# A spectral-mixing and MLP kernel: the first DFT in seven block products per pair of column blocks, all SBUF buffers as views of one tile

## The chip, the cores and the metric

The kernel runs on one core of a Trainium2 chip. The metric is the device time of one execution in microseconds (us). The kernel before takes 1239.16 us, the median of three runs (1237.0 to 1239.35).

The engines are named as in the profile: PE is TensorE's matmul, PEld its weight load, DVE is VectorE, ACT is ScalarE, POOL is GpSimd, SP is SyncE, which issues most of the DMAs.

## The reference

The input x has 2048 rows (S) of 576 (D); the hidden width is 4608. A layer norm feeds two branches, whose results are added to x:

```python
a = jnp.einsum("bsd,ed->bse", x, dft_hid_re)
b = jnp.einsum("bsd,ed->bse", x, dft_hid_im)
y = jnp.einsum("ts,bse->bte", dft_seq_re, a) - jnp.einsum("ts,bse->bte", dft_seq_im, b)
...
h = jnp.einsum("bsd,df->bsf", x, w1)
h = jnp.maximum(h, zero)
return jnp.einsum("bsf,fd->bsd", h, w2)
...
return x + _A_ref(xn, ...) + _B_ref(xn, B_w1, B_w2)
```

The first two lines are the first DFT (over the 576 columns), the third is the second DFT (over the 2048 rows).

## The kernel before

**Arithmetic.** Every float32 operand is scaled by a power of two and split into a high and a low float16 part (`split`: ACT writes the high half, DVE the low one). A product of two matrices is then three float16 products: high by high, high by low, low by high. Where "seven products" are spoken of, a matrix product is cut into 2 x 2 blocks and made of seven block products instead of eight, with sums of blocks made ahead on DVE and sums of results made behind (P1 to P7 in the code).

**Stages.** First come loads, norm and transposes (`xT`: x transposed, float16 high and low, for four groups g of 512 rows). Then the MLP: nine blocks b of 512 hidden columns, each over the four groups; one pair (b, g) is a step. In each step the first layer (L559) and the previous step's second layer (`mlp2`, L665: seven products of 24 matmuls of 288 columns) run on TensorE. ACT and DVE take the results of `mlp2` out of PSUM into sum buffers (L676, L680), and POOL issues a DMA that adds them to a spill in DRAM (L683). In the last block, the sum buffers are `sums`.

The first DFT follows: `dft1(t)` for 16 tiles t of 128 rows, each with four column blocks j of 288 (real columns in two halves, imaginary ones in two). For each tile there are 13 full matmuls for each j (L1252) and a product of 64 rows for what 576 leaves beyond 4 x 128 (L1262, for two tiles at once). The four results lie in four PSUM banks, and the next tile uses four others. ACT and DVE then make of them the operands R of the second DFT: the blocks b11, b21 and b22 and the four sums T1 to T4, each in a high and a low half (L1272 to L1284). The four blocks of the DFT matrix D have a scale each (`scales_d`, `rho`).

The second DFT is 16 units (p, kh) of seven products with 24 matmuls each (L1381): p is a pair of output tiles, kh the half of the 2048 rows that is summed over. Its left operands come from the matrix C (`load_c`: four transfers of 512 KB a unit), split by `operand` three products ahead of use. For the scale of C the absolute values of all its blocks are summed earlier (`first_c`, `sum_c`: a pass over C, one block at a time behind the MLP); four of the 64 blocks are counted during the first DFT instead (`count_c`).

**Order.** `todo` and `work` are a list of small tasks (weights of the next block: load, maximum, scale, splits, sums), taken one by one between the products. `ends` is a list of the last MLP step's remaining conversions. A Tile scheduler puts the instructions on their engines; `behind`, `issue_after` and the order of the code decide what stands behind what.

Buffers come from pools; a pool released and another one opened reuse the same memory, and the later buffer waits for what was in it.

Of the kernel before, what the change touches and what calls it, by code (L numbers as in the profile page):

```python
# [41 lines left out]

BB = 2
# [6 lines left out]
def kernel(  # L50
# [22 lines left out]
    accp = tc.alloc_tile_pool(name="accp", bufs=1)  # L73
    raw = tc.alloc_tile_pool(name="raw", bufs=2)
    mlp = tc.alloc_tile_pool(name="mlp", bufs=2)
    dpool = tc.alloc_tile_pool(name="dpool", bufs=1, side="right")
    xpool = [tc.alloc_tile_pool(name=f"xpool{g}", bufs=1, side="right") for g in range(NG)][::-1]
    ps1 = tc.alloc_tile_pool(name="ps1", bufs=4, space=PSUM)
# [3 lines left out]
    dbuf = dpool.tile([P, 4 * 5 * EH], F32, name="dbuf")  # L82
# [3 lines left out]
    acct = accp.tile([P, NG, TG, D], F32, name="acc")  # L86
    accs = [acct[:, g] for g in range(NG)]
# [9 lines left out]
    stage = mlp.tile([P, 5, NQ, GH], F32, name="stage", bufs=1)  # L97
# [7 lines left out]
    def load_raw(key, src, shape):  # L105
        r = raws[key] = raw.tile(shape, F32, tag="raw", name="raw_" + "_".join(map(str, key)))
        ins = nc.sync.dma_start(r, src).ins
        if key[:2] == ("w2", 1):
            order["loads"] = ins

    def load_w1(b, i, parts=1):
        if b:
            r = raw.tile([P, 2 * KT, P], F32, tag="raw", name=f"raw_w1_{b}_{i}")
        else:
            r = stages[i].rearrange("p (k f) -> p k f", f=P)
# [84 lines left out]
    xT = [xpool[g].tile([P, NKX + 1, G], F16, name=f"xT{g}") for g in range(NG)]  # L200
# [150 lines left out]
    w1bufs = [mlp.tile([P, W1B], F32, name=f"w1buf{i}", bufs=1) for i in range(2)]  # L351
# [37 lines left out]
    def new_h(b, g, i):  # L389
        if i == 0:  # L390
            h = mlp.tile([P, 2, 7, NQ, GH], F16, tag="h", name=f"h{b}_{g}")
# [56 lines left out]
    flats = acct.rearrange("p g a b -> p g (a b)")  # L448
    flat = [flats[:, g] for g in range(NG)]
# [5 lines left out]
    every = acct.rearrange("p g a b -> p (g a b)")  # L455
    cbufs = [
        every[:, k * TG * D - GH : k * TG * D + GH].rearrange("p (i t) -> p i t", i=NQ) for k in (1, 3)
# [180 lines left out]
    sumbufs = [mlp.tile([P, 2, EH], F32, name="sum0", bufs=1)] + [  # L638
# [151 lines left out]
    def new_w2(b, i):  # L790
        w2s[b, i] = mlp.tile([P, 2, 7, EH], F16, tag="w2s", name=f"w2s{b}_{i}", bufs=4)
# [222 lines left out]
    dsp = None  # L1014

    rho = []
    PARTS_D = (slice(0, 3), slice(3, KT))

    def load_d(j):
        load_raw(("d", j), dft[:, :, j * EH : (j + 1) * EH], [P, KT, EH])  # L1020

    def max_d(j, c):

        if j == c == 0:
            sc["d"], pw["d"], mx["d"] = cell("sd", 4), cell("pd", 4), cell("md", 4)
        if c == 0:
            mx["dp"] = cell("mdp", 2)
        with tc.issue_after(order["vfree"]):
            magnitude(mx["dp"][:, c : c + 1], raws["d", j][:, PARTS_D[c]])
        if c:  # L1030
            nc.vector.tensor_reduce(mx["d"][:, j : j + 1], mx["dp"], AX.X, ALU.max)

    def power_d(j):
        m = slice(j, j + 1)
        yield from power(sc["d"][:, m], pw["d"][:, m], mx["d"][:, m])

    def new_d():
        nonlocal dsp
        dsp = [d.bitcast(F16).rearrange("p (n k e) -> p n k e", n=2, k=KT) for d in dbufs]

    def split_d(j, c):
        k = PARTS_D[c]
        with behind("free"), behind("vfree"):
            split(dsp[j][:, 0, k], dsp[j][:, 1, k], raws["d", j][:, k], sc["d"][:, j : j + 1])

    def scales_d():

        top, inv = cell("pdm", 1), cell("pdi", 1)
        nc.vector.tensor_reduce(top, pw["d"], AX.X, ALU.max)
        nc.vector.tensor_scalar(  # L1050
            inv.bitcast(I32), top.bitcast(I32), EXPONENT, None, ALU.bitwise_xor
        )
        r = cell("rho", 5)
        for n, (j, sign) in enumerate(((0, 1), (1, 1), (2, -1), (3, -1), (0, -1))):
            rho.append(r[:, n : n + 1])
            nc.vector.tensor_scalar(
                rho[n], pw["d"][:, j : j + 1], inv, sign * 0.25, ALU.mult, ALU.mult
            )
        pw["d"] = top
# [5 lines left out]
    units = [(p, kh) for p in range(NP) for kh in range(2)]  # L1065
# [9 lines left out]
    def first_c(m):  # L1075
        n, q = divmod(m, 4)
        f = firsts[m] = mlp.tile([P, HK, P], F32, tag="first", name=f"f{n}_{q}", bufs=1)
# [3 lines left out]
    def sum_c(m):  # L1081
# [10 lines left out]
        lambda m=m: (sum_c(m - 1) if m > 4 else None, first_c(m)) for m in range(4, 4 * len(units))  # L1092
# [4 lines left out]
    for n in range(2, len(steps)):  # L1097
        b, g = steps[n]
        pb, pg = steps[n - 1]
        if g == 0 and b:  # L1100
            if b + 1 < NB:
                todo += prepare_block(b + 1)
            else:
                todo += [lambda: (load_d(0), load_d(1)), lambda: None, new_d, lambda: None]
                for j in range(4):
                    d = power_d(j)
                    todo += [lambda j=j: max_d(j, 0), lambda d=d, j=j: (max_d(j, 1), next(d))]
                    todo += [lambda: None, lambda d=d: later(d)]
                    todo += [lambda j=j, c=c: split_d(j, c) for c in range(2)]
                    if j < 2:  # L1110
# [338 lines left out]
```

## Time and profile before

| what | us |
|---|---|
| median of three runs | 1239.16 |
| lowest, highest | 1237.0, 1239.35 |
| profiled execution, its own time | 1238.39 |
| its span (first to last instruction) | 1236.6 |
| stretch of the MLP looked at, blocks in full swing | 440 to 760 |
| the last MLP products, and the first of the first DFT | 784.3 to 797.5 |
| the first DFT | 797.5 to 903.6 |
| the second DFT | 903.6 to 1234.0 |

The granted clock of TensorE is 1.00 in the profiled execution. In the tables of stretches each engine's column is its busy time inside the stretch with its number of instructions in brackets; then come the clock, the mean busy share of the 16 DMA engines and the GB/s that they moved. A row of the groups by form has the busy time of all, the mean of one in ns, and behind the bar the idle time of the engine ahead of them with its releasers. A row of the chain has the start, the duration and what ran. A row of the timeline has the start, the duration and the instruction, with the idle time ahead of it in square brackets.

### The profile page before, as it was taken

The numbers are of one execution on the slowest core, as the hardware profiler recorded it, in microseconds if no ns is written. First come the engines' busy times: TensorE is split into PE (matmuls) and PEld (weight loads), VectorE is DVE, ScalarE is ACT, GpSimd is POOL, SyncE is SP. The second block draws the span as 40 slices with busy tenths as digits, with TensorE's granted clock in tenths as the row PEclk, the third lists the DMA queues.
The fourth block names the chain that finished last, engine by engine and source line by source line (L and its number), as shares of the span: only waits on it lengthen the run. The fifth ranks groups of instructions, "written<-read, shape, count | busy, mean of one in ns | idle before, by whom it ended". The sixth has DMA issues, their size and how long they took to land.

```text
span 1236.6 us, 24680 instructions
## 1 busy us (share of the span) xinstructions
PE 1221.1 (99%) x10269; PEld 965.6 (78%) x10269; DVE 988.3 (80%) x1639; ACT 696.1 (56%) x1024; POOL 158.8 (13%) x208
## 2 busy tenths in 40 slices
PE   8999999999999999999999999999999999999998
PEld 7665657888888888888888888777777777777776
DVE  8998899778877788878877877476887878787875
ACT  5655456676675676666767666445543333333332
POOL 2431211111121212121211111200000000000000
PEclk9999999999999999999999999999999999999999
DMA  8994546657565667576566666620054344433420
GB/s 314 210 162 98 85 70 141 129 125 156 123 141 137 151 132 142 113 157 123 126 149 146 153 134 136 128 69 1 1 175 146 117 130 133 144 119 133 129 88 20
DMA packets 80320, 157.25 MB, mean 127 GB/s; under 512 B 22224, under 2 KB 41168, under 8 KB 80208
## 3 DMA queue, kind: packets, MB, share of 16 engines
q1 hardware_dynamic: 57424, 113.20, 29.4%
q0 software_dynamic: 22784, 42.48, 23.5%
q8 instruction: 80, 1.31, 0.4%
q14 instruction: 32, 0.26, 0.1%
HBM read 104.53 MB, written 51.90 MB: 127 GB/s over the span
## 4 chain that ended last, share of the span: by engine, by line
PE 78%; DVE 11%; issue 5%; DMA 2%; ACT 2%; POOL 1%; SPq 0%; POOLq 0%; ACTq 0%; DVEq 0%
PE p L1381 27%; PE p L665 21%; PE bank L559 19%; PE pd L1252 8%; PE p L356 1%; PE bank L578 1%; DVE h L431 1%; DVE w2s L196 1%; DMA raw_w<-in_w_dram 1%; POOL spill L683 1%; DVE w1buf L196 1%; DMA spill<-sums 1%; DVE h L414 1%; DVE st L219 1%; DVE acc L491 1%
## 5 line engine op out<-in xcount | busy, mean ns | idle before, releaser
L665 PE MATMUL p<-w2s,h 128*128 128x288 f16 x3024 | 399.1, 286 | 4.7 <-DVE acc L680 2.7
L665 PEld LDWEIGHTS <-h 128*128 128x128 f16 x3024 | 295.7, 98 | 81.8 <-issue 6.0
L1381 PE MATMUL p<-R,cs 128*128 128x288 f16 x2688 | 329.4, 286 | 0.0
L1381 PEld LDWEIGHTS <-cs 128*128 128x128 f16 x2688 | 263.0, 98 | 66.3
L195 ACT ACTIVATE cs<-c,sc_c 128x1024 f16<-128x1024 f32 x112 | 125.2, 1144 | 196.7 <-DVE c L1314 72.6
L196 DVE SCALAR_TENSOR_TENSOR cs<-c,sc_c,cs 128x1024 f16<-128x1024 f32 x112 | 141.0, 1282 | 54.4 <-ACT cs L195 54.4
L559 PEld LDWEIGHTS <-w1buf 128*128 128x128 f16 x1476 | 143.0, 98 | 22.5 <-issue 4.4
L559 PEld LDWEIGHTS <-dbuf 128*128 128x128 f16 x1104 | 107.0, 98 | 16.1 <-issue 2.5
L1252 PE MATMUL pd<-dbuf,xT 128*128 128x288 f16 x832 | 104.0, 286 | 0.0
L594 DVE TENSOR_TENSOR h<-stage,h 128x1024 f16<-128x1024 f32 x56 | 68.4, 1223 | 42.2 <-ACT h L590 42.2
L559 PE MATMUL bank<-acc,w1buf 128*128 128x256 f16 x768 | 97.8, 273 | 0.8 <-ACT acc L611 0.8
L1252 PEld LDWEIGHTS <-xT 128*128 128x128 f16 x832 | 80.8, 98 | 22.0 <-issue 1.9
L559 PE MATMUL bank<-xT,w1buf 128*128 128x256 f16 x708 | 95.8, 273 | 0.0
L683 POOL DMA_DIRECT2D spill<-dbuf x70 | 60.6, 872 | 248.0 <-DVE dbuf L680 237.9
L585 ACT ACTIVATE h<-acc 128x512 f16<-128x512 f32 x56 | 35.2, 629 | 75.8 <-DVE acc L615 40.0
L559 PE MATMUL bank<-acc,dbuf 128*128 128x256 f16 x576 | 73.3, 273 | 0.0
L559 PE MATMUL bank<-xT,dbuf 128*128 128x256 f16 x528 | 71.5, 273 | 0.0
L1387 DVE SCALAR_TENSOR_TENSOR o<-p,us_c,o 128x288 f32<-128x288 f32 x112 | 57.5, 513 | 12.9 <-PE p L1381 12.5
L1086 ACT ACTIVATE f<-f 128x1024 f32<-128x1024 f32 x60 | 62.8, 1047 | 3.0 <-DMA f<-in_cre_dram 1.8
L683 POOL DMA_DIRECT2D spill<-sum x42 | 37.3, 889 | 196.1 <-DVE sum L680 172.1
L676 ACT ACTIVATE dbuf<-p,c_ub 128x576 f32<-128x576 f32 x70 | 51.1, 732 | 16.1 <-PE p L665 16.1
L590 ACT ACTIVATE h<-stage 128x1024 f16<-128x1024 f32 x56 | 58.7, 1050 | 0.0
(170 smaller groups left out, 1507.1 us busy)
## 6 DMA issues: line engine op xcount, KB each, us to landing
spill<-dbuf POOLq DMA_DIRECT2D x70, 288.0 KB, 5.8
c<-in_cre_dram SPq DMA_DIRECT2D x32, 512.0 KB, 4.0
c<-in_cim_dram SPq DMA_DIRECT2D x32, 512.0 KB, 4.8
f<-in_cre_dram SPq DMA_DIRECT2D x30, 512.0 KB, 5.1
f<-in_cim_dram SPq DMA_DIRECT2D x30, 512.0 KB, 4.8
spill<-sum POOLq DMA_DIRECT2D x42, 288.0 KB, 4.3
raw_w<-in_w_dram SPq DMA_DIRECT2D x18, 576.0 KB, 4.8
raw_w<-in_w_dram SPq DMA_DIRECT2D x16, 640.0 KB, 5.6
```

The source lines that it names most:

```text
L195: nc.scalar.activation(hi, src, AF.Copy, scale=s).ins,
L196: nc.vector.scalar_tensor_tensor(lo, src, s, hi, ALU.mult, ALU.subtract).ins,
L559: nc.tensor.matmul(ps[:, i], l, r, start=first and i == m == 0, stop=m == len(todo) - 1, skip_group_check=not first or i > 0,)
L590: order["s"] = nc.scalar.activation(h[:, 0, S1 + 2 * i :][:, :2], stage[:, 1 + 2 * i :][:, :2], AF.Copy).ins
L594: order["lo"] = nc.vector.tensor_tensor(lo, stage[:, 1 + 2 * i :][:, :2], hi, ALU.subtract).ins
L665: order["pe"] = nc.tensor.matmul(ps[:, c], h[:, x, qa, c * P : (c + 1) * P], w[:, y, qb], start=first and i == 0 and j == 0, stop=i == NQ ...
L676: freed(nc.scalar.activation(o, ps, AF.Copy, scale=us[b]))
L683: nc.gpsimd.dma_start(spill[g, row, col], o, accum_op=ALU.add)
L1086: nc.scalar.activation(f, f, AF.Abs, scale=2.0**-10, accum_out=sums_c[:, n, q : q + 1])
L1252: nc.tensor.matmul(ps[j], xT[g][:, kx, c * P : (c + 1) * P], dsp[j][:, hl, k], start=(t % 2 == 0 and n == 0), stop=(t % 2 == 1 and n == le ...
L1381: nc.tensor.matmul(ps, w[:, a, k], r[:, c, rq], start=first and k == 0 and j == 0, stop=k == HK - 1 and j == 2, skip_group_check=not first,)
L1387: order["o"] = nc.vector.scalar_tensor_tensor(o, ps, us["c"][:, n : n + 1], o, ALU.mult, ALU.add).ins
```

## The change

**One tile for all buffers.** The pools for SBUF are gone. One tile, `arena`, holds everything; each buffer is a view at an offset worked out by hand (`spots`, `words`), and rings of buffers are taken in turn (`turn`). What waits for what is decided by overlapping ranges, so a later buffer can lie over an earlier one as soon as that is read.

**The first DFT in rounds.** `dft1` is replaced by eight rounds s = (g, c). A round takes two tiles of 128 rows (k = 0, 1) and, for each of two pairs e of column blocks (real, imaginary), seven block products in place of eight. The products stand in PSUM in `U0` and `U1` (one bank each: P1, then P6, then P7, then P4, of e = 0 and of e = 1), `W0` or `W1` (two banks: P5, then P3) and `V` (two banks: P2):

```python
def place(s, e, q):
    if q in (P2, P5, P3):
        return PS["V" if q == P2 else f"W{s % 2}"][:, e]
    return PS[f"U{e}"][:, 0]
def take(s, what, e):
    ...
    if what in ("v", "w", "u"):
        order["dv"] = nc.vector.scalar_tensor_tensor(dst, src, SCALE, dst, ALU.mult, ALU.add).ins
    else:
        order["da"] = nc.scalar.activation(dst, src, AF.Copy, scale=SCALE).ins
```

`take` empties them into a float32 buffer X of the round: c11, r21, c22 and c21 by ACT, and u, w and v are added to what stands there by DVE. `convert` makes R of X: for each of the two tiles the high halves h1, h2, h3a, h3b by ACT, the sums t13, t2, t4 by DVE, the low halves l1, l2 by DVE and l3a, l3b by POOL:

```python
def lo(a, b):
    tt = (nc.gpsimd if a.start > 2 or late_r else nc.vector).tensor_tensor
    tt(r[:, 1, a], x[:, b], r[:, 0, a], ALU.subtract)
```

Part of a round's conversions is made in the next round ("one" is tile k = 1 of this round, "old" the same tile's rest in the next, "late" is tile k = 0 of the round before). The order on the engines is written out as a list and pinned:

```python
else:
    seq = (
        (P1, 0), ("c11", 0), ("late", "h1"), (P1, 1), ("c11", 1), ("old", "t4"), ("old", "l3b"),
        ("old", "h3a"), ("late", "l1"), ("late", "h2"), (P5, 0), ("old", "l3a"), ("late", "l2"),
        ("late", "t13"), (P6, 0), ("r21", 0), ("late", "t2"), ("late", "t4"), (P5, 1),
        ("c22", None), (P6, 1), ("r21", 1), ("late", "h3b"), ("late", "h3a"), (P7, 0), ("u", 0),
        ("late", "l3b"), (P3, 0), (P7, 1), ("u", 1), ("late", "l3a"), ("m", 0),
        (P3, 1), ("rest", 0), ("w", None), ("m", 1), ("m", 2), (P4, 0), ("c21", 0), ("one", "h1"),
        ("one", "l1"), (P4, 1), ("c21", 1), ("one", "h2"), ("one", "l2"), ("one", "t13"), ("one", "t2"),
        (P2, 0), (P2, 1), ("v", None), ("one", "h3b"),
    )
```

("rest" are the eight products of 64 rows, `drests`; "m" stands in the last round alone: the first two operands of the second DFT and one pair of sums of C.)

**The junction.** In round 0 the list alternates with the last MLP step: P1 of e = 0, the MLP's product 0, P5, product 1, P6, product 2, P7, product 3, P3, product 4, P1 of e = 1, product 5, P5, product 6.

**D.** All of D has one scale (and its negative). Its blocks are loaded in two pairs, the second pair twice, six loads of 720 KB in place of four. DVE makes sums of its blocks, and each pair is split into 17 parts of 288 columns in high and low.

**The rest.** The pass over C counts all 64 blocks behind the MLP, with an added place for it in each block's second step; `count_c` is gone. The units of the second DFT come as (0,0), (1,0), (1,1), (0,1), then as before. The last pair's conversions are made in the first unit, two after each product, with all their low halves on POOL.

The diff, cut:

```diff
+    arena = const.tile([P, 4 * W2W + 2 * (HW + RW) + FW + SW + KW + 2 * W1B + 32 + DW + NG * (AW + XW) + 32], F32, name="arena")
...
-    def max_d(j, c):
...
+        r = cell("sd", 2)
+        sc["d"], pw["d"] = [r[:, e : e + 1] for e in range(2)], cell("pd", 1)
+        yield from power(sc["d"][0], pw["d"], m)
+        nc.vector.tensor_scalar(sc["d"][1], sc["d"][0], -1.0, None, ALU.mult)
...
-    units = [(p, kh) for p in range(NP) for kh in range(2)]
+    units = [(0, 0), (1, 0), (1, 1), (0, 1)] + [(p, kh) for p in range(2, NP) for kh in range(2)]
...
-        lambda m=m: (sum_c(m - 1) if m > 4 else None, first_c(m)) for m in range(4, 4 * len(units))
+        lambda m=m: (sum_c(m - 1) if m else None, first_c(m)) for m in range(4 * len(units))
...
-    for q in range(7):
-        mlp2(*steps[-1], q)
-        for _ in range(2):
-            if ends:
-                ends.pop(0)()
...
-        for n, (kx, hl, k) in enumerate(XK[:-1]):
-            for j in range(4):
-                nc.tensor.matmul(
-                    ps[j], xT[g][:, kx, c * P : (c + 1) * P], dsp[j][:, hl, k],
-                    start=(t % 2 == 0 and n == 0), stop=(t % 2 == 1 and n == len(XK) - 2),
-                )
...
+    def dproduct(s, e, q):
+
+        g, c = divmod(s, 2)
+        ps = place(s, e, q)
+        x, a = [y[:, :, c * P : (c + 1) * P] for y in right(g, q)], LEFT[q]
+        first = q in (P1, P2, P5) and (s, e, q) not in opened
+        todo = [
+            (x[z][:, k], dsp(e, y, a + k)) for k in range(2) for y, z in ((0, 0), (1, 0), (0, 1))
+        ]
+        if q in REST:
+            k, t = REST[q]
+            lows = q in (P2, P5) and (s, e, q) not in opened
+            todo += [
+                (xT[g][:, KM, (2 * t + c) * P :][:, :P], dsp(e, y, k)) for y in range(1 + lows)
+            ]
+        for m, (l, r) in enumerate(todo):
+            nc.tensor.matmul(
+                ps, l, r, start=first and m == 0, stop=m == len(todo) - 1,
+                skip_group_check=not first,
+            )
...
+        elif n > 2 and kh and units[n + 1 :]:
+            load_out(units[n + 1][0])
...
+            for _ in range(2):
+                if rest_r:
+                    rest_r.pop(0)()
```

How the change stands on the engines: ACT first. Of the first DFT before, the five instructions of one tile (t = 1); `pd1_0` to `pd1_3` are its four banks, `c12` and `T` float32 buffers, `R1` the operand:

```order
L1272 ACTIVATE c12_1_9825<-pd1_1_9745,c_rho_9375 128x288
L1280 ACTIVATE R1_9771<-pd1_0_9744,c_rho_9375 128x288
L1280 ACTIVATE R1_9771<-pd1_3_9747,c_rho_9375 128x288
L1280 ACTIVATE R1_9771<-pd1_2_9746,c_rho_9375 128x288
L1283 ACTIVATE R1_9771<-T1_9824 128x1152
```

ACT now, in round 2 from its start: U0 (c11 of e = 0), h1 of the late tile, U1 (c11 of e = 1), h3a of the old tile, h2 of the late tile, U0 (r21), W (c22), U1 (r21), h3b and h3a of the late tile, U0 (c21), h1 of this round's tile, U1 (c21). All buffers in SBUF have the one name `arena`:

```order
L1348 ACTIVATE arena_63<-U0_9375 128x288
L1359 ACTIVATE arena_63<-arena_63 128x576
L1348 ACTIVATE arena_63<-U1_9376 128x288
L1359 ACTIVATE arena_63<-arena_63 128x576
L1359 ACTIVATE arena_63<-arena_63 128x288
L1348 ACTIVATE arena_63<-U0_9375 128x288
L1348 ACTIVATE arena_63<-W0_9374 128x576
L1348 ACTIVATE arena_63<-U1_9376 128x288
L1359 ACTIVATE arena_63<-arena_63 128x576 x2
L1348 ACTIVATE arena_63<-U0_9375 128x288
L1359 ACTIVATE arena_63<-arena_63 128x576
L1348 ACTIVATE arena_63<-U1_9376 128x288
```

What moved: an eviction (from U or W) used to follow its own tile's others; now conversions of two other tiles stand between the evictions of one round.

DVE in the first DFT. Before, the eight instructions of tile t = 2:

```order
L1274 SCALAR_TENSOR_TENSOR T2_9908<-pd2_0_9840,c_rho_9375,c12_2_9909 128x288
L1275 SCALAR_TENSOR_TENSOR T2_9908<-pd2_3_9843,c_rho_9375,c12_2_9909 128x288
L1276 SCALAR_TENSOR_TENSOR T2_9908<-pd2_3_9843,c_rho_9375,T2_9908 128x288
L1281 SCALAR_TENSOR_TENSOR R2_9839<-pd2_0_9840,c_rho_9375,R2_9839 128x288
L1277 SCALAR_TENSOR_TENSOR T2_9908<-pd2_2_9842,c_rho_9375,T2_9908 128x288
L1281 SCALAR_TENSOR_TENSOR R2_9839<-pd2_3_9843,c_rho_9375,R2_9839 128x288
L1281 SCALAR_TENSOR_TENSOR R2_9839<-pd2_2_9842,c_rho_9375,R2_9839 128x288
L1284 TENSOR_TENSOR R2_9839<-T2_9908,R2_9839 128x1152
```

And now, round 3 from the late tile's l1 (l1, l2, t13, t2, t4, then the additions u of U0 and U1 and w of W1, then l1, l2, t13 and t2 of the round's own tile):

```order
L1363 TENSOR_TENSOR arena_63<-arena_63 128x576
L1363 TENSOR_TENSOR arena_63<-arena_63 128x288
L1367 TENSOR_TENSOR arena_63<-arena_63 128x2x288
L1375 TENSOR_TENSOR arena_63<-arena_63 128x288
L1376 TENSOR_TENSOR arena_63<-arena_63 128x288
L1346 SCALAR_TENSOR_TENSOR arena_63<-U0_9375,arena_63 128x288
L1346 SCALAR_TENSOR_TENSOR arena_63<-U1_9376,arena_63 128x288
L1346 SCALAR_TENSOR_TENSOR arena_63<-W1_9575,arena_63 128x576
L1363 TENSOR_TENSOR arena_63<-arena_63 128x576
L1363 TENSOR_TENSOR arena_63<-arena_63 128x288
L1367 TENSOR_TENSOR arena_63<-arena_63 128x2x288
L1375 TENSOR_TENSOR arena_63<-arena_63 128x288
```

What moved: the additions from PSUM stand behind five pieces of the round before, and a value is added to in SBUF instead of being worked out from four banks.

POOL, from its last spills to the program's end. Before, one reduction over partitions (for C's scale) ends its work:

```order
L683 DMA spill3_00_107<-sums_8825 128x576
L683 DMA spill3_11_110<-sums_8825 128x576
L683 DMA spill3_01_108<-sums_8825 128x576
L683 DMA spill3_10_109<-sums_8825 128x576
L133 ISA top_10314<-max_c_10312 128x16
L1445 UNCONDITIONAL_BRANCH
L1445 ISA
```

And now:

```order
L717 DMA spill3_01_83<-arena_63 128x576
L717 DMA spill3_10_84<-arena_63 128x576
L1363 ISA
L1363 TENSOR_TENSOR arena_63<-arena_63 128x576 x29
L1363 TENSOR_TENSOR arena_63<-arena_63 128x288 x2
L1363 TENSOR_TENSOR arena_63<-arena_63 128x576 x5
```

What moved: the reduction for C's scale stands ahead of the last seven spills, and behind the last spill come a change of POOL's library (the ISA row) and the 36 low halves.

More of the change, by code (lines that the diff above doesn't have):

```diff
@@ L1133 @@
             t_sum = lambda q: next(tq, None)
+            more = lambda q: g == 1 and count(q)
             rest = lambda q: rests(n + 1 if n + 1 < len(steps) else None)
@@ new lines, with drests @@
+    opened = set()
+    def drests(items):
+        for m, (s, e, q) in enumerate(items):
+            g, c = divmod(s, 2)
+            ps = place(s, e, q)
+            r, kx = m % 2, (KM, NKX)[m % 2]
+            rows = slice(r * REM, (r + 1) * REM)
+            k, t = REST[q]
+            opened.add((s, e, q))
+            nc.tensor.matmul(
+                ps, xT[g][rows, kx, (2 * t + c) * P :][:, :P], dsp(e, 1, k)[rows],
+                start=q in (P2, P5), stop=True, skip_group_check=q not in (P2, P5),
+            )
```

422 lines of the change are left out of this document (262 added, 160 removed).

## The prediction

> **What bounds the kernel now.** I read the page's busy times and its chain first, then a table of stretches, one for each stage, then the chain around the first DFT.
>
> ```profile
> PE 1221.1 (99%) x10269; PEld 965.6 (78%) x10269; DVE 988.3 (80%) x1639; ACT 696.1 (56%) x1024; POOL 158.8 (13%) x208
> PE 78%; DVE 11%; issue 5%; DMA 2%; ACT 2%; POOL 1%; SPq 0%; POOLq 0%; ACTq 0%; DVEq 0%
> ```
>
> ```profile
> core 0: us, PE busy (x) PEld busy (x) DVE busy (x) ACT busy (x) POOL busy (x), PEclk, DMA share, GB/s
> 440.00:760.00 320.00, 320.00 (x2811) 265.93 (x2808) 254.01 (x424) 215.75 (x341) 56.03 (x72) 1.00 0.66 141
> 760.00:784.30 24.30, 23.48 (x204) 19.27 (x202) 18.50 (x35) 14.87 (x24) 4.61 (x7) 1.00 0.52 97
> 784.30:797.50 13.20, 12.29 (x100) 9.47 (x98) 5.71 (x7) 5.89 (x8) 3.52 (x5) 1.00 0.74 136
> 797.50:903.60 106.10, 106.10 (x886) 82.05 (x885) 75.28 (x131) 55.99 (x91) 1.99 (x3) 1.00 0.12 33
> 903.60:1234.00 330.40, 329.32 (x2689) 262.82 (x2686) 261.58 (x290) 123.60 (x113) 0.00 (x0) 1.00 0.38 125
> ```
>
> TensorE is the bound in every stage: 320.00 of 320.00 us in the late MLP blocks, 106.10 of 106.10 in the first DFT, 329.32 of 330.40 in the second. The clock is 1.00 throughout. So a matmul that is left out is worth its full time, and a wait that is put in costs its full time. The one gap beside the change is the junction, 784.3 to 797.5, where 0.9 us of TensorE is idle. The chain shows it and the price of a product:
>
> ```profile
> 730.78 2.94 PE p L665 x24
> ...
> 785.63 8.06 DMA spill<-sums
> ...
> 793.80 0.75 ACT sums L676
> ...
> 794.59 3.10 PE p L665 x24
> 797.69 4.78 PE pd L1252 x39
> 802.47 0.60 PE pd L1262 x8
> 803.07 12.85 PE pd L1252 x104
> ...
> 897.17 6.48 PE pd L1252 x52
> 903.64 329.29 PE p L1381 x2688
> ```
>
> ```profile
> PE p L665 <- ACT sums L676: 0.7, 1, 0.7
> PE p L665 <- ACT h L590: 0.2, 1, 0.2
> ```
>
> A full product costs 12.85/104 = 0.1236 us in the first DFT, a rest product 0.60/8 = 0.075 us.
>
> **What is removed.** The order of instructions has 738 full products in place of 832 and 62 rests in place of 64; up to the junction TensorE's order is the same in both. So 94 x 0.1236 = 11.62 us and 2 x 0.075 = 0.15 us leave a stage that has no idle time: **-11.77**.
>
> **Pace.** Before, successive products go to four banks in turn. Now six or seven in a row stay in one bank, as in the MLP's second layer (2.94/24 = 122.5 ns) and the second DFT (329.29/2688 = 122.5). If that sets the pace, 738 x 1.1 ns = 0.8 us; if not, 0. I take **-0.8**, because these groups are nearest in form.
>
> **Junction.** 0.67 us of the idle time ends with an ACT eviction that waited for a spill of 8.06 us, 0.25 us with an ACT piece of h. Now 47 of the first round's products (5.8 us) stand between the last seven MLP products and need neither. Bounds: 0 to -0.9; I take **-0.9**. The first round's own evictions fall due several microseconds after their products there, so it adds no wait that I can find.
>
> **What is added.** Work per round, of which rounds 1 to 7 have 92 x 0.1236 + 8 x 0.075 = 11.97 us of TensorE:
>
> ```profile
> L195 ACT ACTIVATE w2s<-raw_w,c_sw 128x576 f16<-128x576 f32 x36 | 26.5, 767 | 3.9 <-DVE raw_w L786 2.3 <-DVE raw_w L788 1.4
> L1280 ACT ACTIVATE R<-pd,c_rho 128x288 f16<-128x288 f32 x48 | 24.0, 501 | 21.4 <-DVE T L1274 11.0 <-DVE T L1277 5.2 <-DVE T L1276 5.2
> L605 DVE TENSOR_TENSOR h<-stage,h 128x512 f16<-128x512 f32 x28 | 19.1, 684 | 0.7 <-ACT h L604 0.5
> L280 POOL TENSOR_TENSOR dbuf<-dbuf 128x512 f16<-128x512 f32 x11 | 12.8, 1163 | 0.0
> L676 ACT ACTIVATE sums<-p,c_ub 128x576 f32<-128x576 f32 x16 | 11.8, 736 | 10.4 <-PE p L665 8.6 <-DMA spill<-sums 1.8
> L680 DVE SCALAR_TENSOR_TENSOR sums<-p,c_ub,sums 128x576 f32<-128x576 f32 x12 | 9.8, 813 | 7.5 <-ACT sums L676 3.9 <-PE p L665 3.6
> L786 DVE TENSOR_TENSOR raw_w<-raw_w 128x288 f32<-128x288 f32 x18 | 8.1, 452 | 0.2
> L1276 DVE SCALAR_TENSOR_TENSOR T<-pd,c_rho,T 128x288 f32<-128x288 f32 x16 | 8.1, 508 | 0.0
> ```
>
> ACT: six evictions of 288 (6 x 0.50), one of 576 (0.74), six high halves of 576 (6 x 0.77) and two of 288 (about 0.5 each): 9.4 us. DVE: two additions from PSUM of 288 (0.51), two of 576 (0.81), four SBUF pieces of 576 (0.684 x 576/512 = 0.77) and six of 288 (0.45): 8.4 us. POOL: four low halves of 576, 1.163 x 576/512 = 1.31 each, 5.2 us. No engine is full against 11.97 us, so only order can hurt.
>
> **The new wait.** Two banks, U0 and U1, each take P1, P6, P7 and P4 in turn, so each product but the first needs the eviction of the one before. Before, eight banks went round and nothing had to be empty so soon. From the end of a product to its eviction, and along a chain of ACT and DVE, this part of the trace has:
>
> ```profile
> 856.17 0.67 PE L1262 MATMUL pd<-dbuf,xT 64*128 64x288 f16 x8
> 856.57 0.50 ACT L1272 ACTIVATE c<-pd,c_rho 128x288 f32<-128x288 f32 x1 [1.73 <-PE pd L1262]
> ...
> 859.36 0.50 ACT L1280 ACTIVATE R<-pd,c_rho 128x288 f16<-128x288 f32 x1 [0.35 <-DVE T L1277]
> ```
>
> The eviction at 856.57 reads what the second of eight rests finished at 856.17 + 0.15, so 0.25 us lie between. I laid a round's instructions on the four engines with these durations, counted from its start. P1 ends at 0.74 and 1.48, P6 of the first half ends at 3.09 and of the second at 4.70; P7's first is due at 4.70 into the bank that P6's eviction (r21) frees. P6's first itself waits for the eviction of P1: ACT has it at 1.8 to 2.3, just in time for 2.35, because the previous round's h pieces stand ahead of it. ACT then has two high halves of the previous pair ahead of r21 and ends it at about 4.9: **0.2 us late**. P3 next is due at 5.4 and needs one eviction that ends at 5.5, which the delay covers. The rests are due at 7.9 and need DVE's additions of P7, done at 7.99: nothing more. So +0.2 in seven rounds: **+1.4**. Bounds: 0 if ACT's starts overlap as they do in this trace's rows, and 0.85 a round (+6) if ACT's pieces each cost a 0.35 us start as at 859.36 and two of them stand ahead of r21.
>
> **POOL's new task.** Before its first low half POOL changes its library. The only such gap is
>
> ```profile
> 49.63 0.56 POOL L964 PARTITION_ALL_REDUCE none<-eps  x1 [5.90 <-issue]
> ```
>
> 5.9 us after the last spill is issued (about 802) gives 808; the first low half is wanted by round 1, near 808, and its result only by the second DFT, nearly 100 us later. Cost 0; if the cover failed, X's first half would be rewritten late and one round would wait 2 to 3 us.
>
> **D and its sums.** DVE's splits (34 parts), maxima (8) and seven sums in the last block come to about 23 us, as much as the preparation of an ordinary block's weights, and such blocks run at 320.00 of 320.00. Two more loads of 720 KB fall where the DMA share is 0.52. Cost 0. In block 0 a few pieces of ACT and DVE change places; TensorE has 0.3 us idle there, so I allow 1 us either way:
>
> ```profile
> 60.00:80.00 20.00, 19.67 (x140) 13.50 (x139) 19.44 (x50) 11.84 (x21) 5.42 (x5) 1.00 0.95 136
> ```
>
> **Start of the second DFT.** The last pair's conversions go into the first unit, whose DVE has
>
> ```profile
> 904.00:924.60 20.60, 20.60 (x171) 16.46 (x169) 18.32 (x24) 8.44 (x10) 0.00 (x0) 1.00 0.83 263
> ```
>
> 18.3 us and gets 3.3 more (two pieces of 0.77 and four of 0.45), 21.6 for 20.6. The operands run three products (72 x 0.1225 = 8.8 us) ahead, which swallows 1 us of backlog. Converted rows of the last pair are read one unit later, since the units are reordered. Cost 0; up to +5 if POOL's low halves hold DVE up.
>
> **Sum.** 1238.39 (the profiled execution; its span is 1236.6) - 11.77 - 0.8 - 0.9 + 1.4 = 1226.3. The median of the three runs is 0.77 above that execution, so the forecast is **1227**.
>
> **A rule that speaks against it.** Two rows of block 0 show DVE held by POOL:
>
> ```profile
> 18.56 0.14 DVE L234 SCALAR_TENSOR_TENSOR u<-mv,r 128x2 f32<-128x2 f32 x1
> 23.92 1.16 POOL L280 TENSOR_TENSOR dbuf<-dbuf 128x512 f16<-128x512 f32 x1
> 24.27 0.82 DVE L234 SCALAR_TENSOR_TENSOR u<-mv,r 128x4 f32<-128x4 f32 x1
> ```
>
> The same small operation takes 0.14 us alone and 0.82 us when it begins inside a POOL piece, and both end together at 25.08. The Trainium skill, "SBUF — State Buffer", section "SBUF: two separate sides", says that the port pair shared by the two engines is an exclusive lock, so that a DVE operation with two SBUF inputs waits for the whole of a GpSimd one; the trace agrees with 0.82 against 0.14.
>
> **The rivals.** (1) Everything is hidden, no wait at r21: 1238.39 - 13.5 + 0.8 = 1225.7. For it: ACT's pieces in this trace overlap by 0.1 us each; against: r21's slack is negative on paper.
>
> (2) DVE and POOL exclude each other, and DVE becomes the chain of the round. Then 8.4 + 5.2 = 13.6 us, and with a start of 0.35 us at some two of its hand-overs 14.3, stand against 11.97: 2.3 us a round, 16 in seven, and 1238.39 - 13.5 + 16.3 + 0.8 = **1242, slower**. It decides from 13.5/7 = 1.9 us of wait a round. For it: the rows above. Against: DVE's pieces that read PSUM have one SBUF input only, the low halves are wanted by nobody within the round, and POOL's four pieces start when ACT's halves are done, which leaves DVE free in between.
>
> (3) The second DFT starts late: DVE's backlog, POOL's locks and 2 MB of C with the spilled rows arrive together. 5 us on the forecast, 1232. For it: 0.83 of the DMA there already; against: three products of lead.
>
> (4) The change does not bring its count: the products would have to take 832 x 123.6/738 = 139 ns to give back all. Nothing in the trace is near it; 1239.
>
> **How the numbers follow.** Forecast 0.61 (own range 1224.5 to 1230), (1) 0.13, (3) 0.14, (2) 0.09, (4) 0.03. About 0.2 per cent, 2.5 us, is the least that a measurement of this kernel tells from no change. Faster: 0.61 + 0.13 + 0.14 = 0.88; same 0.03; slower 0.09. The range goes from 1224 (all bounds low and block 0 a little better) to 1236 (0.85 us a round, or a late second DFT with more than 5): that leaves out (2), (4) and little else.
>
> **What would show it.** Right: 738 full products at about 122.5 ns, rounds of 12.1 to 12.2 us, a wait of 0.2 us in each before P7, named ACT; no idle TensorE near 788 and 794; the second DFT still at 329 of 330. Wrong: waits of a microsecond or more before the rests, named DVE, with DVE pieces stretched beside POOL ones (rival 2); idle TensorE within 20 us after the last round (rival 3); idle in the MLP's blocks, which I hold to be untouched.

## The result, and the profile after

| | before | after |
|---|---|---|
| median of 20 runs | 1239.16 | 1237.97 |
| lowest, highest | 1237.0, 1240.55 | 1235.75, 1239.27 |
| span of the profiled execution | 1236.6 | 1235.9 |

The ratio is 0.999 (95% interval 0.9983 to 0.9996): 1.2 us faster, where 12.2 were forecast (1227). The time lies above the range's upper end, 1236.

First the page of the kernel after, the busy times:

```profile
PE 1211.0 (98%) x10173; PEld 956.2 (77%) x10173; DVE 999.4 (81%) x1619; ACT 707.2 (57%) x1073; POOL 210.2 (17%) x241
```

TensorE does 10.1 us less (1221.1 before), 96 matmuls fewer, and the span is only 0.7 us shorter: nearly all of the gain came back as idle time of TensorE. The table of stretches says in which stages (the columns are as before):

```profile
760.00:784.30 24.30, 20.95 (x181) 17.16 (x179) 18.00 (x26) 15.20 (x24) 3.46 (x4) 1.00 0.61 140
784.30:797.50 13.20, 13.03 (x108) 10.30 (x106) 10.22 (x15) 6.80 (x13) 3.97 (x5) 1.00 0.52 82
...
903.60:1234.00 330.40, 324.30 (x2641) 258.18 (x2639) 264.47 (x289) 121.89 (x112) 10.13 (x5) 1.00 0.35 116
```

From 760 to 784.3 TensorE is idle for 3.4 us (0.8 before), from 903.6 on for 6.1 us (1.1 before); 1.4 and 1.1 us of these lie behind the last product. The junction is nearly full. The single waits are in TensorE's timeline of the kernel after (start, duration, instruction, idle time ahead and its releaser; only the rows with a wait are shown):

```profile
775.19 1.47 PE L593 MATMUL bank<-arena 128*128 128x256 f16 x12 [1.07 <-ACT arena L647]
782.04 0.40 PE L612 MATMUL bank<-arena 64*128 64x256 f16 x4 [2.29 <-DVE arena L649]
791.06 1.63 PE L699 MATMUL p<-arena 128*128 128x288 f16 x12 [0.17 <-DVE arena L714]
821.00 0.28 PE L1328 MATMUL U<-arena 64*128 64x288 f16 x1 [0.16 <-DVE arena L1346]
897.66 6.04 PE L1555 MATMUL p<-arena 128*128 128x288 f16 x48 [0.50 <-ACT arena L1348]
905.16 6.04 PE L1555 MATMUL p<-arena 128*128 128x288 f16 x48 [1.45 <-DVE arena L1561]
911.86 3.10 PE L1555 MATMUL p<-arena 128*128 128x288 f16 x24 [0.67 <-DVE arena L1561]
916.44 3.10 PE L1555 MATMUL p<-arena 128*128 128x288 f16 x24 [1.48 <-DVE arena L1561]
920.11 17.80 PE L1555 MATMUL p<-arena 128*128 128x288 f16 x144 [0.57 <-DVE arena L1561]
938.41 294.16 PE L1555 MATMUL p<-arena 128*128 128x288 f16 x2400 [0.50 <-DVE arena L1561]
```

The rounds themselves hold no wait but the 0.16 us at 821. The sum of the two profiled executions closes so: work -11.77; junction -0.75 (0.92 to 0.17); rounds +0.16; last MLP block +2.5 (1.07 + 2.29 against 0.82); start of the second DFT +5.2 (the last six rows; none before); waits ahead of 500 us +2.4 (12.37 against 9.94, of which more below); and some 0.16 us for each of nine more restarts after a wait (a row of 48 ahead of a wait lasts 6.04 where 48 x 0.1225 is 5.88), +1.4. Together -0.8; the spans differ by 0.7.

**The second DFT's start.** DVE and POOL in the first unit, two timelines of the kernel after, DVE's first:

```profile
893.84 2.03 DVE L230 SCALAR_TENSOR_TENSOR arena<-arena,sc_c 128x1024 f16<-128x1024 f32 x1 [1.05 <-ACT arena L229]
...
897.65 2.29 DVE L1409 TENSOR_TENSOR arena<-arena 128x1024 f32<-128x1024 f32 x1
...
919.98 1.87 DVE L230 SCALAR_TENSOR_TENSOR arena<-arena,sc_c 128x1024 f16<-128x1024 f32 x1
```

```profile
892.27 2.52 POOL L1363 TENSOR_TENSOR arena<-arena 128x576 f16<-128x576 f32 x2 [2.27 <-ACT arena L1359]
897.39 4.82 POOL L1363 TENSOR_TENSOR arena<-arena 128x576 f16<-128x576 f32 x3 [2.60 <-ACT arena L1359]
...
912.85 7.92 POOL L1363 TENSOR_TENSOR arena<-arena 128x576 f16<-128x576 f32 x4 [7.04 <-ACT arena L1359]
```

Without POOL beside them the same two operations of DVE take 1.27 and 1.21 us (quoted below). The one at 893.84 takes 0.76 us more and ends at 895.87, which is 1.08 us after POOL's pair ends (892.27 + 2.52 = 894.79). The one at 919.98, of the same form, ends at 921.85, again 1.08 us after POOL's last piece (912.85 + 7.92 = 920.77). Though they lie beside POOL's piece for 0.95 and 0.79 us, nearly all of their work, 1.08 of 1.27 us, is done behind it; engines that only slowed each other down would have done a part of it before (as far as POOL's spans, which are rough, tell). The one at 897.65 ends at 899.94; if POOL's first of three took 1.26 us, as each of the pair at 892.27 did, it ended at 898.65, and 1.29 us are left for DVE's. POOL waits too: four pieces in a row take 7.92 us, 1.98 each, against those 1.26.

**The last MLP block.** The second load of D's imaginary columns, ACT's timeline of the kernel after, and three rows of DVE's:

```profile
770.92 1.01 ACT L229 ACTIVATE arena<-arena,c_sd 128x864 f16<-128x864 f32 x1 [3.46 <-DMA arena<-in_dft_dram]
...
778.64 0.78 ACT L229 ACTIVATE arena<-arena,c_sd 128x576 f16<-128x576 f32 x1 [2.55 <-DMA arena<-in_dft_dram]
779.32 0.61 ACT L619 ACTIVATE arena<-arena 128x512 f16<-128x512 f32 x1
```

```profile
764.48 0.81 DVE L230 SCALAR_TENSOR_TENSOR arena<-arena,c_sd 128x576 f16<-128x576 f32 x1
...
767.13 0.81 DVE L230 SCALAR_TENSOR_TENSOR arena<-arena,c_sd 128x576 f16<-128x576 f32 x1
...
781.30 0.68 DVE L649 TENSOR_TENSOR arena<-bank,arena 128x512 f32<-128x512 f32 x1
```

ACT stands still for 3.46 and 2.55 us with a split of D at its head, and behind it stand the pieces of h (L619) that DVE's eviction L649 comes after; TensorE's 2.29 us end with that eviction. The load could not start before 765.4 and 768.0, since it goes where the real columns lie until they are split: DVE's splits at 764.48 and 767.13 end at 765.29 and 767.94. SP's timeline shows its issues right behind, with one block of C between them, and the chain what the second took:

```profile
765.36 0.55 SPq L141 DMA_DIRECT2D arena<-in_dft_dram  x1
765.96 0.62 SPq L1132 DMA_DIRECT2D arena<-in_cre_dram  x1
767.97 0.55 SPq L141 DMA_DIRECT2D arena<-in_dft_dram  x1
```

```profile
767.97 10.64 DMA arena<-in_dft_dram
```

That is the longest of D's six loads, whose median is 7.4 us. So the second wait of ACT has two parts, a late start and a slow transfer.

### The profile page after: what moved, and what is told of

Its sections match the earlier page's. It is cut to its first block, busy times and chain, and to the rows that moved or that the text cites. A ratio compares the mean times of both kernels' runs of the same rounds, so it can differ in the third digit from the quotient of the medians.

```text
span 1235.9 us, 24513 instructions
## 1 busy us (share of the span) xinstructions
PE 1211.0 (98%) x10173; PEld 956.2 (77%) x10173; DVE 999.4 (81%) x1619; ACT 707.2 (57%) x1073; POOL 210.2 (17%) x241
## 3 DMA queue, kind: packets, MB, share of 16 engines
q8 instruction: 79, 1.29, 0.4%
## 4 chain that ended last, share of the span: by engine, by line
PE 73%; DVE 15%; issue 5%; ACT 3%; DMA 3%; POOL 0%; SPq 0%; ACTq 0%; POOLq 0%; DVEq 0%
PE p L1555 24%; PE p L699 22%; PE bank L593 19%; DVE arena L230 3%; PE U L1312 3%; PE W L1312 2%; DMA arena<-in_w_dram 1%; PE p L392 1%; DVE arena L714 1%; PE bank L612 1%; ACT arena L229 1%; DVE arena L468 1%; DMA arena<-in_dft_dram 1%; PE V L1312 1%; DVE arena L451 1%
## 5 line engine op out<-in xcount | busy, mean ns | idle before, releaser
L699 PE MATMUL p<-arena 128*128 128x288 f16 x3024 | 400.2, 286 | 5.8 <-DVE arena L714 5.7
L699 PEld LDWEIGHTS <-arena 128*128 128x128 f16 x3024 | 295.8, 98 | 83.5 <-issue 8.4
L1555 PE MATMUL p<-arena 128*128 128x288 f16 x2688 | 330.2, 286 | 5.2 <-DVE arena L1561 4.7
L1555 PEld LDWEIGHTS <-arena 128*128 128x128 f16 x2688 | 263.0, 98 | 72.4 <-issue 6.3
L593 PE MATMUL bank<-arena 128*128 128x256 f16 x2580 | 304.8, 273 | 1.2 <-ACT arena L647 1.1
L593 PEld LDWEIGHTS <-arena 128*128 128x128 f16 x2580 | 250.1, 98 | 39.1 <-issue 7.6
L229 ACT ACTIVATE arena<-arena,sc_c 128x1024 f16<-128x1024 f32 x112 | 124.3, 1144 | 199.5 <-DVE arena L1410 75.3
L717 POOL DMA_DIRECT2D spill<-arena x144 | 128.6, 911 | 553.4 <-DVE arena L714 504.5
L230 DVE SCALAR_TENSOR_TENSOR arena<-arena,sc_c 128x1024 f16<-128x1024 f32 x112 | 144.3, 1312 | 51.8 <-ACT arena L229 51.8
L710 ACT ACTIVATE arena<-p,c_ub 128x576 f32<-128x576 f32 x144 | 105.5, 734 | 43.3 <-PE p L699 38.2
L230 DVE SCALAR_TENSOR_TENSOR arena<-arena,c_sw 128x640 f16<-128x640 f32 (+2 forms) x118 | 98.2, 847 | 24.8 <-ACT arena L229 24.5
L229 ACT ACTIVATE arena<-arena,c_sw 128x640 f16<-128x640 f32 (+3 forms) x118 | 90.3, 795 | 23.1 <-DVE c_sw L171 10.8
L392 PE MATMUL p<-arena 128*128 128x128 f16 (+1 forms) x680 | 98.5, 300 | 1.8 <-ACT arena L347 1.1
L1312 PEld LDWEIGHTS <-arena 128*128 128x128 f16 x738 | 71.6, 98 | 19.7 <-issue 1.9
L392 PEld LDWEIGHTS <-arena 128*128 128x128 f16 x680 | 52.3, 98 | 40.3 <-issue 3.8
L619 ACT ACTIVATE arena<-arena 128x512 f16<-128x512 f32 x56 | 35.2, 628 | 67.7 <-DVE arena L649 39.7
```

The lines of the kernel that those rows point to most:

```text
L229: nc.scalar.activation(hi, src, AF.Copy, scale=s).ins,
L230: nc.vector.scalar_tensor_tensor(lo, src, s, hi, ALU.mult, ALU.subtract).ins,
L392: order["m1"] = nc.tensor.matmul(ps[:, cols], w1s[b, i // 2][:, hl, i % 2 * KT + k], xT[g][:, kx, cols], start=(start and n == 0), stop=(s ...
L593: nc.tensor.matmul(ps[:, i], l, r, start=first and i == m == 0, stop=m == len(todo) - 1, skip_group_check=not first or i > 0,)
L699: order["pe"] = nc.tensor.matmul(ps[:, c], h[:, x, qa, c * P : (c + 1) * P], w[:, y, qb], start=first and i == 0 and j == 0, stop=i == NQ ...
L710: freed(nc.scalar.activation(o, ps, AF.Copy, scale=us[b]))
```

## The experiments

Theory 1: at the start of the second DFT, DVE has more than it can do, and POOL's hold on it is the larger part. Theory 2: in the last MLP block ACT and DVE wait, at the head of their queues, for a load that starts late. Theory 3: the extra slot of the pass over C costs about 1 us in the earlier blocks. The rivals: plain work of DVE for 1 and 2, and differences from execution to execution for 3.

**u1_late**: the last pair's conversions in the second unit.

```diff
-            for _ in range(2):
+            for _ in range(4 if n == 1 else 0):
                 if rest_r:
-                    rest_r.pop(0)()
+                    with tc.issue_after(order["o"]), tc.issue_after(order["oa"]):
+                        rest_r.pop(0)()
```

(`order["oa"]` is ACT's half of the last operand's split, so that the pieces keep their place on ACT too. In the kernel after nothing pins the pieces: its code has 14 of the 22 behind the first unit's products and eight behind the second's, but on the engines all stand in the first unit, where POOL's last ends at 920.77.)

> The last pair's conversions (22 pieces) move from the first unit of the second DFT, two after each product, to the second unit, four after each product; nothing is left out. Theory 1 (in the first unit DVE has more than it can do: the pieces themselves and the low halves on POOL, which hold DVE's operations up): TensorE's idle time in the first unit falls from 5.2 us to under 1 us, and the time from 1238.0 to about 1232.5 (5.2 us of idle time and some 0.16 us for each of the five restarts). Rival (the operands are late for another reason, such as C's loads or the spilled rows): 3 us or more of idle time stay in the first unit, and the time is 1236 or more.

Measured 1238.16, ratio to before 0.9991 (0.9982 to 0.9999): no gain over the kernel after (1237.97). But the waits moved with the pieces. TensorE's timeline and the stretches of u1_late:

```profile
932.71 3.10 PE L1555 MATMUL p<-arena 128*128 128x288 f16 x24 [1.11 <-DVE arena L1561]
937.58 8.98 PE L1555 MATMUL p<-arena 128*128 128x288 f16 x72 [1.77 <-DVE arena L1561]
948.28 8.98 PE L1555 MATMUL p<-arena 128*128 128x288 f16 x72 [1.72 <-DVE arena L1561]
957.75 4.45 PE L1555 MATMUL p<-arena 128*128 128x288 f16 x35 [0.50 <-DVE arena L1561]
```

```profile
900.00:921.00 21.00, 20.30 (x165) 15.94 (x164) 18.06 (x22) 8.62 (x9) 1.21 (x1) 1.00 0.46 146
921.00:942.00 21.00, 18.11 (x147) 14.13 (x146) 17.66 (x21) 8.84 (x11) 12.22 (x8) 1.00 0.29 101
```

The first unit now loses 0.6 us; the second loses 2.9 (the first two rows) and the third, whose operands are made beside the last pieces, 2.2. So C's loads are not the cause, since the first unit still has them; the pieces are. The expectation's 1232.5 was wrong in taking the second unit to have room for them.

**u0_nolow** and **u0_nosums** part the pieces. The first leaves out the eight low halves on POOL, the second DVE's six sums:

```diff
-            tt(r[:, 1, a], x[:, b], r[:, 0, a], ALU.subtract)
+            if not late_r:
+                tt(r[:, 1, a], x[:, b], r[:, 0, a], ALU.subtract)
```

```diff
-    rest_r = [d[k] for d in (old, late) for k in keys]
+    rest_r = [d[k] for d in (old, late) for k in keys if k[0] != "t"]
```

> The eight low halves of the last two tiles, which POOL writes in the first unit of the second DFT, are left out; the other 14 pieces stay where they are. If POOL's hold on DVE is the larger part of theory 1: DVE's operands in the first unit take 1.2 to 1.3 us each again in place of 1.6 to 2.3, idle time at most 1.5 us, time about 1233 to 1234. If DVE's own added sums (3.3 us) are the larger part: 3 us or more of idle time stay and the time is 1236 or more.

> The six sums t13, t2, t4 of the last pair (3.3 us of DVE) are left out, the low halves on POOL stay. Theory 1a (POOL's hold on DVE is the larger part): 2 to 3.5 us of the 5.2 us of idle time in the first unit stay, 1235 to 1236.5. Theory 1b (it is the sum of both that overflows, and either alone fits): idle time under 1.5 us, time 1232 to 1233.5.

Measured 1231.76 (ratio 0.9939, 0.9925 to 0.9952) and 1237.59 (0.9987, 0.9978 to 0.9997). TensorE's waits at the start of the second DFT, from the list of waits of u0_nolow, and from the timeline of u0_nosums:

```profile
PE p L1556 <- ACT arena L1348: 0.5, 1, 0.5
PE p L1556 <- DVE arena L1562: 0.5, 1, 0.5
```

```profile
898.79 6.04 PE L1555 MATMUL p<-arena 128*128 128x288 f16 x48 [1.51 <-ACT arena L1348]
907.36 6.04 PE L1555 MATMUL p<-arena 128*128 128x288 f16 x48 [2.53 <-DVE arena L1561]
914.17 3.10 PE L1555 MATMUL p<-arena 128*128 128x288 f16 x24 [0.77 <-DVE arena L1561]
917.92 2.24 PE L1555 MATMUL p<-arena 128*128 128x288 f16 x17 [0.66 <-DVE arena L1561]
```

Without POOL's pieces 1.0 us is left of 5.2; without DVE's 3.3 us of sums 5.5 us is left, more than theory 1a asked for, and 1237.59 lies above the ranges of both 1a and 1b. The sums alone are not the loss; the hold makes nearly all of it. In u0_nosums the low halves also come in another order: all eight run in one string of 14.39 us on POOL, beside DVE's operands.

**u01_dve** and **u01_spread**: nothing left out, the 22 pieces spread over two units, with the pins of u1_late; in the first DVE makes the low halves, in the second POOL still does. They differ in that line alone.

```diff
-            for _ in range(2):
+            for _ in range((1, 1, 1, 2, 2, 2, 2)[i] if n == 0 else 2):
...
-            tt = (nc.gpsimd if a.start > 2 or late_r else nc.vector).tensor_tensor
+            tt = (nc.gpsimd if a.start > 2 and not late_r else nc.vector).tensor_tensor
```

> Nothing is left out. The last pair's low halves are made by DVE instead of POOL (5.5 us more of DVE, no hold), and the 22 pieces are spread over the first two units of the second DFT. By the durations of the rows DVE has 2 x 16.6 + 3.3 + 5.5 = 42 us for 41.2: idle time of 1 to 2.5 us, time 1238.0 - 3 to 4.5 = 1233.5 to 1235. If the hold were not the matter: as u1_late, 1237 to 1238.5.

> Nothing is left out. The 22 pieces are spread over the first two units, the low halves still on POOL. Theory 1 with a hold of up to 1.3 us for each of eight POOL pieces: DVE has 33.2 + 3.3 + 6 to 10 = 42.5 to 46.5 us for 41.2, idle time 1.5 to 5 us, 1234 to 1238. Rival (only the bunching in one unit matters): idle time under 1 us, 1232.5.

Measured 1233.29 (0.9953, 0.9936 to 0.9969) and 1237.65 (0.999, 0.9981 to 0.9999). The first gives DVE some 5.4 us more work than the second gives it (six pieces of 0.75 us and two of 0.44), and is 4.4 us faster: TensorE waits 1.1 us at the start of its second DFT, 5.4 us in u01_spread. So bunching alone is not the cause either; spread out, POOL's pieces cost as much. Stretches of 25 us from the start of the second DFT, of the kernel after and of u01_dve, then two rows of u01_dve's DVE:

```profile
897.00:922.00 25.00, 20.33 (x162) 15.58 (x160) 24.97 (x25) 11.85 (x15) 15.10 (x8) 1.00 0.54 186
```

```profile
898.00:923.00 25.00, 24.38 (x199) 19.29 (x198) 24.03 (x29) 12.68 (x14) 0.00 (x0) 1.00 0.53 179
```

```profile
896.68 1.27 DVE L230 SCALAR_TENSOR_TENSOR arena<-arena,sc_c 128x1024 f16<-128x1024 f32 x1
897.87 1.21 DVE L1409 TENSOR_TENSOR arena<-arena 128x1024 f32<-128x1024 f32 x1
```

In the kernel after DVE shows 24.97 of 25.00 us busy with 25 instructions, in u01_dve 24.03 us with 29, at their plain durations: a full DVE in a profile may be a DVE that waits inside its instructions.

**d_noreload** and **d_late2** test theory 2. The first leaves out the second load of D's imaginary columns; the second, with nothing left out, splits them later:

```diff
-                todo += prepare_d(0) + [lambda: load_d(1), lambda: None] + prepare_d(1)[:DA]
+                todo += prepare_d(0) + [lambda: None] * 2 + prepare_d(1)[:DA]
```

```diff
-    DA = 5
+    DA = 2
...
-                todo += prepare_d(0) + [lambda: load_d(1), lambda: None] + prepare_d(1)[:DA]
+                todo += prepare_d(0) + [lambda: load_d(1)] + [lambda: None] * 4 + prepare_d(1)[:DA]
...
-                (P5, 0), ("c22", 0), ("mlp", 1), ("tail", 0), (P6, 0), ("r21", 0), ("mlp", 2), ("tail", 0),
-                (P7, 0), ("u", 0), ("mlp", 3), ("tail", 0), (P3, 0), ("mlp", 4), ("tail", 0),
+                (P5, 0), ("c22", 0), ("tail", 0), ("mlp", 1), ("tail", 0), ("tail", 0), (P6, 0), ("r21", 0), ("mlp", 2), ("tail", 0), ("tail", 0),
+                (P7, 0), ("u", 0), ("mlp", 3), ("tail", 0), (P3, 0), ("mlp", 4), ("tail", 0),
```

> The second load of the imaginary columns of D (two of 720 KB) is left out, so that their parts are made of what the first sums left there. Theory 2 (ACT and DVE stand behind a split that waits for that load, and the first layer's evictions behind them): TensorE's waits of 1.1 and 2.3 us in the last MLP steps shrink to 0.8 us or less in all, and the time goes from 1238.0 to about 1235. Rival (the added sums and splits of D are simply too much for DVE there): both waits stay, 1237.5 to 1238.5.

> Nothing is left out. The parts of D's imaginary columns are split later: four empty tasks behind their second load in place of one, and of the five early pieces only two; the other eight stand between the last seven MLP products. Theory 2 (the load is waited for at the head of ACT's and DVE's queues): the waits of 1.1 and 2.3 us near 775 and 782 shrink to 1 us or less in all, and unless the pieces are late for the first round (then new waits between 790 and 810), the time is 1238.0 - 3 to 5 = 1233 to 1235. Rival (the work itself is too much): the waits move to the junction, 1237 to 1239.

Measured 1232.62 (0.9949, 0.9933 to 0.9964) and 1234.09 (0.996, 0.9945 to 0.9975). In both no wait of TensorE is left between 500 and 800 us, and the second DFT's waits stay what they were; the list of waits of d_late2:

```profile
PE p L1555 <- DVE arena L1561: 4.7, 5, 1.5
```

So it was the splits that wait for the load at the head of the queue, not D's work, which d_late2 does in full, nor the load itself: the longest of the loads by L141 still takes 10.0 us there. d_noreload gained some 2 us more than expected; a part of that may lie in the waits ahead of 500 us, which differ between executions as the next run shows.

**before_more**: the kernel before with the extra slot of the pass over C.

```diff
+            more = lambda q: g == 1 and count(q)
...
-                (run, P6), (end, 0), (end, 0), (run, P2), (t_sum, 0), (m, 1), (used, P2), (ready, 1),
+                (run, P6), (end, 0), (end, 0), (run, P2), (t_sum, 0), (m, 1), (used, P2), (more, 0), (ready, 1),
```

> The kernel before with one edit of the change alone: the pass over C takes one block more in the second step of each MLP block. Theory 3 (each added piece of 1.2 us on ACT, or its transfer, delays the weights' splits where the MLP has little slack): one or two new waits of 0.5 to 1 us between 200 and 500 us, time 1239.2 + 0.7 to 1.7 = 1240 to 1241. Rival (the waits seen there in the changed kernel differ from run to run, as a load of 5.4 or 6.4 us does): no new step there, 1239.2 within 0.5.

Measured 1238.73, ratio 0.9996 (0.9987 to 1.0005): theory 3 falls at the size that it gave. Its list of waits has two that the kernel before lacked or had smaller:

```profile
PE bank L578 <- DVE acc L615: 1.2, 1, 1.2
PE p L665 <- ACT sum L676: 1.1, 1, 1.1
```

All waits ahead of 500 us add up to 11.8 us in this execution, against 9.9 in that of the kernel before, 12.4 in that of the kernel after and 10.2 (d_noreload) to 13.9 (d_late2) in those of its variants. So the +2.4 of my sum there may for the most part be the difference of two single executions; one profile of each kernel can't say how much. A small real cost of the slot may be seen near 207 us, where before_more and every changed kernel have waits of 0.3 and 1.2 us and the kernel before has one of 1.0 us. One wait looks systematic and stays open: near 448 us, 0.2 to 0.9 us in the profiled executions of the changed kernel and of all its variants but d_late2, and in neither of the kernel before and before_more.

**both_1** joins d_late2 and u01_dve; **both_2** is the same with the pieces of the first unit one product later.

> The edits of d_late2 and of u01_dve together; nothing is left out. If the late load of D and POOL's hold on DVE are two separate losses, their gains add: 1238.0 - 3.9 - 4.7 = 1229.4 (1228.5 to 1230.5), with no idle time in the last MLP block or the junction and about 1 us in the second DFT. If one hides behind the other: 1231.5 or more.

> As both_1, with the pieces of the last pair one product later and one fewer at the fourth product. If the 1 us left in the second DFT comes of pieces in front of the first operands: 0.3 to 1 us less than both_1. If it comes of the operands that stand in the last round: the same as both_1 within 0.4 us.

Measured 1228.24, ratio to before 0.991 (0.9896 to 0.9923), and 1228.67 (0.9915, 0.9901 to 0.9928). The two gains add, with some to spare: both_1 is 9.7 us below the kernel after, where 3.9 and 4.7 were found alone. It came out just under the expected range, and what the last 1.1 us are stays open. Stretches of both_1, the last MLP block, the junction, and the first two units:

```profile
760.00:784.30 24.30, 24.30 (x213) 20.21 (x212) 18.23 (x26) 16.09 (x25) 4.58 (x6) 1.00 0.60 137
784.30:797.50 13.20, 13.20 (x110) 10.56 (x108) 11.04 (x17) 9.04 (x14) 2.77 (x4) 1.00 0.77 130
...
890.00:932.00 42.00, 40.79 (x331) 32.13 (x329) 41.02 (x51) 21.83 (x25) 0.09 (x1) 1.00 0.54 171
```

TensorE is full in the first two. In the units 1.2 us is left, and DVE is busy for 41.02 of 42 us with POOL all but idle; shifting pieces by one product (both_2) did not help, which fits a DVE that is full of its own work. both_1 is 11.0 us faster than the kernel before, with nothing left out, and beats both kernels.

## Why the prediction was wrong

**The work removed** (-11.77) was right to 0.1 us (94 products at the 0.1225 us found below are 11.52 in place of 11.62), and it came: both_1 has it.

**Pace** (-0.8) was wrong. In the kernel before, a string of 39 products with no rests in it took 4.78 us, 122.6 ns each, and the prediction quoted that row. The 123.6 ns were 12.85 us for 104, of which 0.11 us is the change from the rests to the full products; eight such changes there are now as before. The term should have been 0. The rows of one round in the chain of the kernel after:

```profile
833.28 0.22 PE U L1328
...
833.88 1.82 PE U L1312 x14
835.70 1.72 PE V L1312 x14
837.41 1.47 PE U L1312 x12
...
845.25 0.23 PE U L1328
```

12 products take 1.47 us, 122.5 ns each, the first 14 behind the rests 0.1 us more than the next 14, and the round 11.97 us, just its work.

**Junction** (-0.9): right in kind, -0.75 in the profile.

**The new wait** (+1.4, r21 0.2 us late in each round) did not come; the rounds have 0.16 us in all, and that ahead of the rests. Groups by form of the kernel after:

```profile
L1359 ACT ACTIVATE arena<-arena 128x576 f16<-128x576 f32 x48 | 31.7, 677 | 23.8 <-DVE arena L1375 20.7 <-DVE arena L1376 2.5 <-DVE arena L1346 0.6
L1348 ACT ACTIVATE arena<-U 128x288 f32<-128x288 f32 x48 | 19.4, 404 | 15.5 <-PE U L1312 12.7 <-PE U L1328 2.3
```

An eviction takes 0.40 us and a high half 0.68, where I had taken 0.50 and 0.77 from rows with a scale held in SBUF; here the scale is a constant or none. I had no row for that form, and 0.1 us at each piece ahead of r21 is about the 0.2 us; this is worked out from the rows, no run tried it. Pace made the forecast 0.8 us too low and this term made it 1.2 us too high; that the two nearly cancel is luck.

**POOL's library** (0) and **the sum of both engines in the rounds**: right. In the rounds DVE is held as well (its low halves of 288 columns take 0.91 us on average, 0.44 in u01_dve's second DFT), but it has room, and TensorE waits for 0.16 us there, 0 to 0.8 us in the variants. The rival of the exclusive ports, as put, was to decide in the rounds; it did not.

**D and its sums** ("Cost 0") is one of the two steps that failed. It counted the work of DVE, which fits, and the mean share of the DMA engines, and left out that the second load could not start until the real columns were split, and that each split stands at the head of ACT's queue in front of the MLP's own pieces. Cost 2.5 us more in the waits of this block than before; d_late2, which takes away all of its 3.4 us and the junction's rest, gains 3.9. The sign that the prediction named, idle time in the MLP's blocks, did come.

**Start of the second DFT** ("Cost 0; up to +5 if POOL's low halves hold DVE up") is the other. The bound was nearly right (5.2 us of idle time and about 1 us of restarts; u01_dve, with all the work done, gains 4.7, and u0_nolow, which leaves work out, 6.2), the value was not: 21.6 us of work for 20.6 were weighed against the 8.8 us by which operands run ahead, but the operands' own pieces read two SBUF operands, and POOL's eight low halves met them. The rows of block 0 that showed the hold stood in the prediction. They were worked out for the rounds alone, where there was room; for the unit that was already over-full they gave only the bound and a part of rival 3. Rival 3 named the place at 0.14; the case that came, rival 3 and a late load together, was in none of them, and each alone stays within the range: with only the hold left the time is 1234.09 (d_late2), with only the late load 1233.29 (u01_dve).

**The earlier blocks**: the prediction allowed 1 us either way in block 0 and held the rest of the MLP to be untouched; the two profiled executions differ by 2.4 us ahead of 500 us, and the runs don't settle how much of that is the change.

## What to carry to other kernels

Weigh a POOL piece beside DVE as DVE time where DVE is nearly full, and as free only where DVE has room: low halves on POOL left TensorE 0.16 us of waits in the rounds and 5.2 us at the start of the second DFT. For a load into memory that is still read, work out its start from the last reader, and look at what stands behind its first user in that engine's queue, not at the mean load of the DMA engines. A gain that vanishes can be eaten by two stalls in stages beside the one that was rewritten; a table of TensorE's idle time by stage finds them faster than the changed stage itself.

## What the runs showed of the hardware

DVE and POOL excluded each other for whole instructions: a DVE operation of 1.21 us took 2.29 us when POOL's began 0.26 us ahead of it, two of 1.27 us ended 1.08 us after the POOL piece in which they had begun, and four POOL pieces of 1.26 us took 7.92 us beside a busy DVE. This is what the Trainium skill says in "SBUF — State Buffer", section "SBUF: two separate sides", and the runs agree with it: with POOL's pieces taken away (u0_nolow) or made by DVE itself (u01_dve), DVE's operations with no POOL piece beside them were back at 1.21 and 1.27 us. Not expected was that DVE alone did both engines' work sooner than the two side by side (1233.29 against 1237.65).
